# A decode step of attention and MLP: x and y made stationary for q and h, P widened to 64, a diagonal picked by masked sums, and `wo` loaded in 4-row runs

## The chip, the cores and the metric

The kernel runs on one core of a Trainium2 chip. The metric is the device time of one execution in microseconds, given as the median of the executions of a kernel with the lowest and the highest beside it. For a program on one core, "slow" is a run over 1.5% above the fastest of the same kernel.

## The reference, cut to what matters

Eight rows of one token each go through attention over the last 2048 positions of a cache (16 KV heads, two query heads each, 128 wide) and, beside it, through a GELU MLP; a sigmoid gate mixes the two.

```python
# x: 8 x 1 x 576; k_cache, v_cache: 8 x 16 x 8192 x 128; W = 2048; all bf16
q = x @ wq                                            # 576 x 4096
k, v = repeat(k_cache[:, :, Sk-W:]), repeat(v_cache[:, :, Sk-W:])
p = softmax(einsum("bhqd,bhkd->bhqk", q, k) * Dh**-0.5)
a = einsum("bhqk,bhkd->bhqd", p, v).reshape(...) @ wo   # 4096 x 576
b = gelu(layernorm(x) @ w1 + b1) @ w2 + b2            # 576 -> 4608 -> 576
return g * a + (1 - g) * b                            # g = sigmoid(sum(x * gate_w))
```

K and V in the window are 134 MB of the 154 MB that are read.

## The kernel before

One stream of loads on the sync engine fills nine slots of 2 MB in the order K, V, K, V, with four pieces of `wo` between and `w2` at the end. A K unit or V unit is one slot: four batch rows of one head. Four K units make a group with one softmax; there are eight groups. A K unit is transposed on VectorE in two halves, and each half feeds 8 matmuls on TensorE. A V unit does three things on TensorE's side: the PV matmuls, an eviction of their result by ScalarE, and a closing sum, which picks the useful diagonal out of the result.

A small planner inside the kernel fixes, at build time, the order of the instructions on every engine from modelled durations. On the chip each engine runs its own list in that order and waits at semaphores. The change and the argument touch these parts:

```python
def pv_fn(e):                                   # 16 matmuls, P stationary, 32 wide
    for t in range(16):
        c = 32 * (t % 4)
        mm = e.matmul(ps[c:c+32, BK_OS[i % 2], :], PT[...32*t : 32*t+32], slot(s)[:, 512*t:512*t+512], ...)
prev = add("pe", pv_fn, deps=[d] + pt_done[g] + [u_ev[i - 2]], cost=1.5, after=pv_hist[-1:])   # cut
u_ev[i] = add("act", ... activation(out=EV[:, i % 2, :], in_=ps[:, BK_OS[i % 2], :]), deps=[prev, u_sum[i - 2]])

def us_fn(e):                                   # closing sum: 4 fp32 matmuls on the diagonal blocks
    for r in range(4):
        mm = e.matmul(ps[...8 columns], EV[:, i % 2, 128*r:128*r+128], i32[:, 8*r:8*r+8], start=(r == 0), stop=(r == 3))
u_sum[i] = add("pe", us_fn, deps=[u_ev[i]] + ..., cost=1.0, prio=3)
# ...
# softmax of a group (cut): row maximum, exp, transposes of P, then
ds = add("dve", ... tensor_scalar(out=dsum, in0=i32, scalar1=k(S), op0=mult))       # 128 x 32
sp_ = add("pe", ... matmul(ps[:, BK_S, 0:32], ones_f, dsum))                        # sum of the group
# ...
d = dma("sp", ... A_wo[128*h0:128*(h0+8), :].rearrange("(t p) c -> p t c", p=128))  # rows of 1152 bytes
```

Of the kernel before, what the change touches and what calls it, by code (L numbers as in the profile page):

```python
# [179 lines left out]
def build_kernel(nc, A_x, A_k_cache, A_v_cache, A_wq, A_wo, B_x, B_w1, B_b1, B_w2, B_b2, gate_w, out):  # L180
# [16 lines left out]
    WOP = 768  # L197
# [7 lines left out]
    with ExitStack() as es:  # L205
# [19 lines left out]
        req("zeros_bf", 128, BF)  # L225
        req("maskL", 128, BF)
# [4 lines left out]
        req("sel", 4 * 128, BF)  # L231
        req("cols", 16, F32)
        req("xT", 6 * 8, BF)
        req("yT", 6 * 8, BF)
# [18 lines left out]
        req("EV", 2 * 512, F32)  # L253
        req("oT", Hkv * 16, BF)
        req("out_sb", JN, BF)
# [12 lines left out]
        over("sq", "KT", 2304, D, F32)  # L268
        arena = es.enter_context(nc.sbuf_tensor("arena", [128, (aoff[0] + 1) // 2], BF))
# [25 lines left out]
        sel = view("sel").rearrange("p (h c) -> p h c", h=4)  # L295
        cols = view("cols")
        xT = view("xT").rearrange("p (t b) -> p t b", b=8)
        yT = view("yT").rearrange("p (t b) -> p t b", b=8)
# [13 lines left out]
        o32 = view("o32").rearrange("p (u m) -> p u m", u=2)  # L312
        oT = view("oT").rearrange("p (u h b) -> p u h b", u=Hkv, h=2)
        out_sb = view("out_sb")
# [26 lines left out]
        BK_Q, BK_H, BK_X, BK_SEL = 4, 5, 6, 0  # L341
        BK_OS = (4, 5)
# [25 lines left out]
        o_selb = []  # L368
        for he in range(4):
            def fn(e, he=he):  # L370
                src = bass.AP(arena, offset=aoffs("ident") + 64 * (he // 2) + he % 2, ap=[[AST, 128], [0, 4], [2, 32]])
                return e.tensor_copy(sel[:, he, :].rearrange("p (a i) -> p a i", a=4), src)
            o_selb.append(add("pool", fn, deps=[o_ident], name="selb%d" % he, cost=0.3))
# [62 lines left out]
        def ev_T(dst, which):  # L436
            return lambda e: e.tensor_copy(dst, ps_bf[:, BK_X, which * 64: which * 64 + 48].rearrange("p (t b) -> p t b", b=8))
        o_xT = add("dve", ev_T(xT, 0), deps=[o_b1p], name="xT_ev", cost=0.2)
# [8 lines left out]
        o_yT = add("dve", ev_T(yT, 1), deps=[o_gp, o_yTp], name="yT_ev", cost=0.2)  # L447
# [6 lines left out]
        for q in range(4):  # L454
            o_i32.append(add("dve", (lambda q=q: lambda e: e.tensor_copy(i32[32 * q:32 * q + 32, :], ident[32 * q:32 * q + 32, 32 * q:32 * q + 32]))(),
                             deps=[o_ident, o_obl], name="i32_%d" % q, cost=0.15, prio=-1))


        def q_fn(e):
            ins = None  # L460
            for hq in range(Hq):
                out_ = ps[:, BK_Q, hq * 8: hq * 8 + 8]
                for t in range(4):
                    ins = e.matmul(out_, wq_m[:, t, hq * 128:(hq + 1) * 128], xT[:, t, :], start=(t == 0), stop=False)
                c = hq % 16
                ins = e.matmul(out_, wq_r[:, c * 128:(c + 1) * 128], xT[:, 4 + hq // 16, :], start=False, stop=True)
            return ins
        o_qp = add("pe", q_fn, deps=dwq + [o_xT], name="q_pe", cost=9.0)

        def qT_fn(e):  # L470
            src = bass.AP(ps, offset=BK_Q * 512, ap=[[PST, 128], [16, 16], [1, 8], [8, 2]])
            return e.tensor_copy(view("qT").rearrange("p (l b h) -> p l b h", l=16, b=8), src)
        o_qT = add("dve", qT_fn, deps=[o_qp], name="qT_ev", cost=0.4)

        def sel_fn(e):
            ins = None
            for he in range(4):
                ins = e.matmul(ps[:, BK_SEL + he // 2, (he % 2) * 256:(he % 2) * 256 + 256], sel[:, he, :], view("qT"), start=True, stop=True)
            return ins
        o_selp = add("pe", sel_fn, deps=[o_qT] + o_selb, name="sel_pe", cost=0.6, prio=9)  # L480

        def q4_fn(e):
            return e.activation(out=view("q4"), in_=ps[:, BK_SEL:BK_SEL + 2, :].rearrange("p a n -> p (a n)"), func=ACTF.Copy)
# [3 lines left out]
        H_CH = 6  # L487
        o_hch = []
        for i0 in range(0, FT, H_CH):
            fts = list(range(i0, min(FT, i0 + H_CH)))  # L490
            def fn(e, fts=fts):
                ins = None
                for t in fts:
                    c, j = divmod(t, FJ)
                    out_ = ps[:, BK_H, t * 8: t * 8 + 8]
                    for kt in range(4):
                        lhsT = bass.AP(arena, offset=aoffs("RAW") + W1O + kt * F + FCW * c + j, ap=[[AST, 128], [FJ, 128]])
                        ins = e.matmul(out_, lhsT, yT[:, kt, :], start=(kt == 0), stop=False)  # L498
                    lhsT = bass.AP(arena, offset=aoffs("RAW") + W1O + 4 * F + FCW * (c % 2) + j, ap=[[AST, 128], [FJ, 128]])
                    ins = e.matmul(out_, lhsT, yT[:, 4 + c // 2, :], start=False, stop=True)  # L500
                return ins
            o_hch.append(add("pe", fn, deps=dw1 + [o_yT], name="h_pe%d" % len(o_hch), cost=0.06 * 5 * len(fts), after=o_hch[-1:]))
        o_hp = o_hch[-1]

        def u_fn(e):
            in1 = bass.AP(arena_f, offset=foffs("b1T"), ap=[[AST // 2, 128], [1, FT], [0, 8]])
            return e.tensor_tensor(out=u_sb.rearrange("p (t b) -> p t b", b=8), in0=ps[:, BK_H, 0:FT * 8].rearrange("p (t b) -> p t b", b=8), in1=in1, op=ALU.add)
        GC = math.sqrt(2.0 / math.pi)
        o_u = add("dve", u_fn, deps=[o_hp, o_b1T], name="u", cost=0.45)
# [13 lines left out]
        def acc0_fn(e):  # L523
            ins = None
            for j in range(NJ):
                ins = e.matmul(ps[32 * j:32 * j + 32, BK_ACC, 0:JN], zeros_bf[:, 0:32], maskR[:, 0:JN], start=True, stop=True,
                               skip_group_check=True, tile_position=(0, 32 * j))
            return ins
        o_acc0 = add("pe", acc0_fn, deps=[o_z, o_mR], name="acc0", cost=0.5)
        acc_groups = []  # L530

        class AccGroup:
            def __init__(self, name, mms, deps, cost, after=(), prio=0):
                grp = self
                self.mms = mms

                def fn(e):
                    ins = None
                    for i, (lhsT, rhs) in enumerate(grp.mms):
                        for j in range(NJ):  # L540
                            ins = e.matmul(ps[32 * j:32 * j + 8, BK_ACC, 0:JN], lhsT, rhs[:, JN * j:JN * j + JN], start=False, stop=True,  # L541
                                           skip_group_check=True, tile_position=(0, 32 * j))
                    return ins
                self.op = add("pe", fn, deps=deps, name=name, cost=cost, after=list(after) + [o_acc0], prio=prio)
# [25 lines left out]
        u_ev, u_sum = {}, {}  # L570
        b6_w, b6_r = [], [o_yT, o_gb]
        proj_ops = {}
# [51 lines left out]
        def k_unit(i):  # L624
# [13 lines left out]
            for h in range(2):  # L638
# [23 lines left out]
                if q == 0 and h == 0:  # L662
                    deps += exp_done[g - 1] if g else [o_q4, o_mL, o_mR]
# [7 lines left out]
        def v_unit(i):  # L671
# [6 lines left out]
            def pv_fn(e):  # L678
                mm = None
                for t in range(16):  # L680
                    c = 32 * (t % 4)
                    mm = e.matmul(ps[c:c + 32, BK_OS[i % 2], :], PT[:, g % 2, 512 * q + 32 * t:512 * q + 32 * t + 32], slot(s)[:, 512 * t:512 * t + 512],  # L682
                                  start=(t < 4), stop=(t >= 12), skip_group_check=True, tile_position=(0, c))
                return mm
            deps = [d] + pt_done[g] + ([u_ev[i - 2]] if i >= 2 else [o_qT, o_u])
            prev = add("pe", pv_fn, deps=deps, name="pv%d" % i, cost=1.5, after=pv_hist[-1:])
            pv_hist.append(prev)
            slot_free[s] = [prev]
            if q == 3:
                pv_last[g] = prev  # L690
            u_ev[i] = add("act", lambda e: e.activation(out=EV[:, i % 2, :], in_=ps[:, BK_OS[i % 2], :], func=ACTF.Copy),  # L691
                          deps=[prev] + ([u_sum[i - 2]] if i >= 2 else []), name="uev%d" % i, cost=0.8, prio=3)

            def us_fn(e):
                mm = None
                for r in range(4):
                    mm = e.matmul(ps[:, BK_S, OC + 16 * (item % 2) + 8 * (q % 2):OC + 16 * (item % 2) + 8 * (q % 2) + 8], EV[:, i % 2, 128 * r:128 * r + 128], i32[:, 8 * r:8 * r + 8],  # L697
                                  start=(r == 0), stop=(r == 3), skip_group_check=True)
                return mm
            u_sum[i] = add("pe", us_fn, deps=[u_ev[i]] + o_i32 + b6_r[-2:], after=b6_w[-1:], name="us%d" % i, cost=1.0, prio=3)  # L700
# [18 lines left out]
        def wo_chunk(i):  # L719
            s = take_slot()  # L720
            h0 = WO_CH * i
            dst = slot(s)[:, 0:WO_CH * WOP].rearrange("p (t c) -> p t c", t=WO_CH)
            d = dma("sp", lambda e: e.dma_start(dst[:, :, 0:D], A_wo[128 * h0:128 * (h0 + WO_CH), :].rearrange("(t p) c -> p t c", p=128)),
                    "s%d" % s, WO_CH * 128 * D * 2, deps=slot_free[s], name="d_wo%d" % i, after=last_dma[-1:])
            last_dma.append(d)
# [112 lines left out]
```

## Time and profile before

The time was 369.55 us (369.44 to 369.65, three runs). The prediction shows the slices, the chain and the DMA stretches. In all profile lines PE is TensorE, PEld its weight loads, DVE VectorE, ACT ScalarE, POOL GpSimd and SP the sync engine; L691 is line 691 of the kernel that was run, so the same operation has another line number in each kernel.

Between a PV (L682) and its closing sum (L697) lies one eviction of 0.6 us, and TensorE hardly stands for it: 0.7 us at most. Its large waits are for the softmax (L606, the transposes of P) and for the transposed K (L642).

| | kernel before |
|---|---|
| busy of TensorE, VectorE, GpSimd | 72%, 57%, 10% |
| row maxima of groups 3 to 8 start at | 123.2, 165.1, 205.0, 246.4, 286.8, 328.3 us |
| that is, one group takes | 41.9, 39.9, 41.4, 40.5, 41.5 us |

### The profile page before, as it was taken

How to read it: one execution, taken by the hardware profiler on the slowest of the kernel's cores; microseconds unless marked ns; L12 is line 12 of the kernel's file. 1: busy time of each engine (PE TensorE's matmuls, PEld its weight loads, DVE VectorE, ACT ScalarE, POOL GpSimd, SP SyncE). 2: the span in 40 equal slices, each digit the busy share in tenths (PEclk: the TensorE clock that was granted, in tenths of full speed). 3: DMA queues.
4: the chain of work that ended last, by engine and by line, in shares of the span. 5: the costliest groups of instructions: out<-in, count | busy, mean ns of one | idle time of the engine just before them, and what ended most of it. 6: DMA issues, size and time to landing. Idle time of an engine off the chain costs nothing.

```text
span 367.9 us, 4129 instructions
## 1 busy us (share of the span) xinstructions
PE 263.5 (72%) x1837; PEld 87.0 (24%) x1429; DVE 210.4 (57%) x253; ACT 47.8 (13%) x117; POOL 37.5 (10%) x163
## 2 busy tenths in 40 slices
PE   0349984797698589773986399774976398773984
PEld 0339200122132022110321032110321032113542
DVE  0704599699686665459654674469544775364000
ACT  1010000210300220003000310003100300003200
POOL 7020011012011002000101002010110000000000
PEclk9999999699599869887897869886996879886659
DMA  8999999999999999999999999999999999999994
GB/s 345 428 412 424 435 430 433 428 428 428 433 429 431 422 433 426 428 435 427 433 431 433 408 434 432 429 426 433 433 436 428 414 434 424 431 433 440 402 429 193
DMA packets 14923, 154.59 MB, mean 420 GB/s; under 512 B 1292, under 2 KB 5428, under 8 KB 6072
## 3 DMA queue, kind: packets, MB, share of 16 engines
q1 hardware_dynamic: 14848, 154.29, 98.9%
q8 instruction: 13, 0.21, 0.2%
q10 hardware_dynamic: 56, 0.03, 0.0%
q14 instruction: 6, 0.05, 0.0%
HBM read 154.31 MB, written 0.01 MB: 419 GB/s over the span
## 4 chain that ended last, share of the span: by engine, by line
DMA 61%; PE 20%; DVE 16%; SPq 1%; issue 1%; ACT 0%; DVEq 0%; ACTq 0%
DMA arena<-in_A_k_cache_dram 50%; DMA arena<-in_B_w_dram 11%; DVE arena L642 10%; PE ps L173 9%; PE ps L659 3%; DVE arena L587 3%; PE ps L498 2%; PE ps L682 2%; PE ps L697 2%; DVE arena L606 1%; DVE arena L590 1%; PE ps L500 1%; SPq L675 1%; DVE arena L596 0%; SPq L746 0%
## 5 line engine op out<-in xcount | busy, mean ns | idle before, releaser
L642 DVE STREAM_TRANSPOSE arena<-arena 128x2048 f32<-128x2048 f32 x64 | 145.5, 2299 | 71.1 <-DMA arena<-in_A_k_cache_dram 60.1
L173 PE MATMUL ps<-arena 128*128 128x512 bf16 x408 | 141.3, 462 | 0.0
L659 PE MATMUL ps<-arena 128*128 128x512 bf16 x128 | 58.8, 459 | 21.4 <-DVE arena L642 21.3
L691 ACT ACTIVATE arena<-ps 128x512 f32<-128x512 f32 x32 | 19.1, 598 | 196.8 <-PE ps L682 196.8
L659 PEld LDWEIGHTS ps<-arena 128*128 128x128 bf16 x128 | 15.0, 117 | 124.6 <-issue 71.3
L635 POOL COPY arena<-arena 32x32 bf16<-32x32 bf16 x128 | 26.0, 203 | 159.8 <-PE ps L173 145.2
L697 PE MATMUL ps<-arena 128*128 128x8 f32 x256 | 35.3, 269 | 8.7 <-ACT arena L691 7.7
L697 PEld LDWEIGHTS ps<-arena 128*128 128x128 f32 x256 | 34.0, 208 | 21.8 <-ACT arena L691 15.2
L682 PE MATMUL ps<-arena 128*32 128x512 bf16 x512 | 36.4, 410 | 2.9 <-DMA arena<-in_A_v_cache_dram 2.9
L651 PE MATMUL ps<-arena 128*128 128x512 bf16 x8 | 4.7, 585 | 40.8 <-DVE arena L606 40.8
L587 DVE TENSOR_REDUCE arena<-ps 128x1 f32<-128x2048 f32 x8 | 18.3, 2282 | 21.6 <-PE ps L173 21.6
L601 ACT ACTIVATE arena<-ps,arena 128x512 bf16<-128x512 f32 x32 | 21.6, 686 | 40.9 <-DVE arena L596 40.9
L606 DVE STREAM_TRANSPOSE arena<-arena 128x512 bf16<-128x512 bf16 x32 | 19.9, 674 | 0.9 <-ACT arena L601 0.9
L682 PEld LDWEIGHTS ps<-arena 128*32 128x32 bf16 x512 | 11.3, 100 | 37.4 <-issue 27.1
L715 POOL TENSOR_TENSOR arena<-arena 128x16 bf16<-128x16 f32 x15 | 4.0, 266 | 141.7 <-ACT arena L707 141.7
L498 PE MATMUL ps<-arena 128*128 128x8 bf16 x144 | 10.9, 201 | 4.7 <-DMA arena<-in_B_w_dram 4.7
L541 PE MATMUL ps<-arena 128*8 128x288 bf16 (+1 forms) x140 | 11.9, 316 | 2.9 <-DMA arena<-in_B_w_dram 2.8
L498 PEld LDWEIGHTS ps<-arena 128*128 128x128 bf16 x144 | 10.8, 157 | 5.2 <-DMA arena<-in_B_w_dram 5.2
L651 PEld LDWEIGHTS ps<-arena 128*128 128x128 bf16 x8 | 0.9, 107 | 45.1 <-DVE arena L606 45.1
L613 DVE RECIPROCAL arena<-ps 128x32 f32<-128x32 f32 x8 | 2.9, 358 | 13.9 <-PE ps L611 13.9
L420 PE MATMUL ps<-arena 8*128 8x8 bf16 x8 | 0.5, 167 | 13.4 <-DVE arena L393 9.7
L715 DVE TENSOR_TENSOR arena<-ps,arena 128x16 bf16<-128x16 f32 x1 | 0.2, 229 | 16.7 <-PE ps L697 16.7
(83 smaller groups left out, 97.1 us busy)
## 6 DMA issues: line engine op xcount, KB each, us to landing
arena<-in_A_k_cache_dram SPq DMA_DIRECT2D x32, 2048.0 KB, 33.3
arena<-in_A_v_cache_dram SPq DMA_DIRECT2D x32, 2048.0 KB, 34.1
arena<-in_B_w_dram SPq DMA_DIRECT2D x1, 4608.0 KB, 24.3
arena<-in_A_wo_dram SPq DMA_DIRECT2D x4, 1152.0 KB, 36.6
arena<-in_A_wq_dram SPq DMA_DIRECT2D x1, 4096.0 KB, 13.0
arena<-in_B_w_dram SPq DMA_DIRECT2D x3, 1296.0 KB, 14.8
arena<-in_B_w_dram SPq DMA_DIRECT2D x2, 576.0 KB, 20.6
arena<-in_A_wq_dram SPq DMA_DIRECT2D x1, 512.0 KB, 3.6
```

The lines of the kernel that those rows point to most:

```text
L173: return e.add_instruction(mybir.InstMatmult(name=nc.get_next_instruction_name(), engine=mybir.EngineType.PE, ins=[e.lower_ap(rhs), e.lowe ...
L498: ins = e.matmul(out_, lhsT, yT[:, kt, :], start=(kt == 0), stop=False)
L541: ins = e.matmul(ps[32 * j:32 * j + 8, BK_ACC, 0:JN], lhsT, rhs[:, JN * j:JN * j + JN], start=False, stop=True, skip_group_check=True, til ...
L587: mx = add("dve", lambda e: e.tensor_reduce(out=k(MX), in_=ps[:, 0:4, :].rearrange("p a n -> p (a n)"), axis=AXL.X, op=ALU.max), deps=[qk_ ...
L601: return e.activation(out=Pm[:, 512 * c:512 * c + 512], in_=ps[:, c, :], func=ACTF.Exp, bias=k(NB), scale=SCALE, accum_out=k(SUM + c))
L606: pts.append(add("dve", (lambda c=c: lambda e: e.transpose(bass.AP(arena, offset=aoffs("PT") + 2048 * (g % 2) + 128 * c, ap=[[AST, 128], [ ...
L635: return e.tensor_copy(dst, src)
L642: tr = add("dve", (lambda h=h, kb=kb: lambda e: e.transpose(bass.AP(arena_f, offset=foffs("KT") + kb * 2048, ap=[[AST // 2, 128], [1, 2048]]),
L659: mm = e.matmul(*args, start=False, stop=last) if rc == 0 else held_matmul(nc, e, *args, stop=last)
L682: mm = e.matmul(ps[c:c + 32, BK_OS[i % 2], :], PT[:, g % 2, 512 * q + 32 * t:512 * q + 32 * t + 32], slot(s)[:, 512 * t:512 * t + 512], st ...
L691: u_ev[i] = add("act", lambda e: e.activation(out=EV[:, i % 2, :], in_=ps[:, BK_OS[i % 2], :], func=ACTF.Copy), deps=[prev] + ([u_sum[i - ...
L697: mm = e.matmul(ps[:, BK_S, OC + 16 * (item % 2) + 8 * (q % 2):OC + 16 * (item % 2) + 8 * (q % 2) + 8], EV[:, i % 2, 128 * r:128 * r + 128 ...
```

## The change

It means to take work off TensorE's instruction stream (fewer, wider matmuls for q, h, PV and the closing sum) and to load `wo` in longer runs. The core of the diff, with cuts marked:

```diff
 # q and h: x and y (x after layernorm) become the stationary operand, weights are streamed 512 or 288 wide
-            for hq in range(Hq): ... 5 matmuls, wq stationary, xT[:, t, :] moving
+            for t in range(5): for n in range(2): for j in range(4): ... xT stationary, wq moving
+        o_qx = add("dve", ... transpose of 128 x 1024 ...)
 # ... (h in the same way)
-                for t in range(16):   # PV: P 32 wide, V 512 wide, two banks in turn
+                for t0 in range(0, 8, 2): for dh in range(2): for t in (t0, t0 + 1):   # P 64 wide, V in two d halves
-            deps = [d] + pt_done[g] + [u_ev[i - 2]]
+            deps = [d] + pt_done[g] + u_ev[i - 1]        # both banks are used by every unit now
+            for dh in range(2): u_ev[i].append(add("act", ...))            # two evictions
+            re = "dve" if i >= NUQ - 3 else "pool"
+            um = add(re, ... EV * m8 ...)                                  # masked multiply, 128 x 1024 fp32
+            for n in (512, 256, 128): um = add(re, ... EV[0:n] + EV[n:2n])  # three adds (GpSimd only; VectorE: one strided reduce)
             def us_fn(e):
-                for r in range(4): ... EV block, i32
+                return e.matmul(..., E1[:, i % 2, :], s8)                  # one closing matmul
-    A_wo[...].rearrange("(t p) c -> p t c", p=128)
+    A_wo[...].rearrange("(g p t) c -> p g (t c)", g=2, t=4)                # runs of 4608 bytes
+    for hh in range(4): for t in range(4): ... add("dve", tensor_copy oT -> oTp)   # permutation, 16 per piece
```

## The prediction

> **What bounds the kernel now.** I read the page's slices first, then the chain that ended last, then the DMA rate in stretches around each load of `wo`, then the sync engine's issues and the last microseconds of the timeline.
>
> The slices of the page:
>
> ```profile
> span 367.9 us, 4129 instructions
> PE 263.5 (72%) x1837; PEld 87.0 (24%) x1429; DVE 210.4 (57%) x253; ACT 47.8 (13%) x117; POOL 37.5 (10%) x163
> ...
> DMA  8999999999999999999999999999999999999994
> GB/s 345 428 412 424 435 430 433 428 428 428 433 429 431 422 433 426 428 435 427 433 431 433 408 434 432 429 426 433 433 436 428 414 434 424 431 433 440 402 429 193
> DMA packets 14923, 154.59 MB, mean 420 GB/s; under 512 B 1292, under 2 KB 5428, under 8 KB 6072
> ```
>
> No compute engine is above 72%, while the 16 DMA engines are full from the first slice to the next to last. 154.59 MB at a steady 430 GB/s is 359.5 us; 2.2 us of start, 2 to 3 us of landing, last matmuls, eviction and store, and some slower slices make up the rest of 367.9. The bytes set the time; this change moves the same bytes.
>
> The chain seems to say otherwise:
>
> ```profile
> DMA 61%; PE 20%; DVE 16%; SPq 1%; issue 1%; ACT 0%; DVEq 0%; ACTq 0%
> ```
>
> It gives 36% to PE and DVE. That is how it walks: from a landing back to what freed the slot. While a slot is being freed, six or seven other loads wait in the queue (a K or V load takes a median 33.3 or 34.1 us from issue to landing, though 2 MB need 4.9 us). I take the DMA row as the verdict. Compute matters only if it uses up that lead: the shortest landings are 20.1 us for K and 16.2 us for V, so about 11 us are to spare even at the tightest place.
>
> The DMA rate in stretches (columns: stretch, length, busy of PE, PE loads, DVE, ACT, POOL with counts, clock, DMA share, GB/s):
>
> ```profile
> 90.00:124.00 34.00, 28.32 (x166) 7.61 (x115) 22.21 (x27) 4.84 (x13) 3.57 (x17) 0.80 1.01 431
> 124.00:135.00 11.00, 4.87 (x16) 0.45 (x4) 10.07 (x19) 3.38 (x9) 0.21 (x1) 0.73 1.02 417
> 135.00:205.00 70.00, 53.42 (x326) 15.00 (x235) 39.12 (x36) 7.71 (x19) 6.75 (x32) 0.85 1.01 430
> 205.00:217.00 12.00, 5.88 (x28) 0.91 (x15) 10.84 (x19) 3.38 (x9) 0.81 (x4) 0.75 1.04 423
> 217.00:286.00 69.00, 53.14 (x319) 14.92 (x227) 39.12 (x35) 7.71 (x19) 6.74 (x32) 0.85 1.00 429
> 286.00:300.00 14.00, 7.87 (x46) 1.70 (x37) 11.32 (x21) 3.38 (x9) 0.82 (x4) 0.76 1.03 424
> 300.00:340.00 40.00, 29.01 (x194) 10.29 (x145) 20.91 (x26) 6.03 (x15) 0.53 (x2) 0.84 1.01 431
> 340.00:353.00 13.00, 11.59 (x97) 7.14 (x97) 0.00 (x0) 2.76 (x6) 0.54 (x2) 0.63 1.02 416
> ```
>
> The four `wo` loads are issued at 95.7, 178.4, 259.9 and 314.8 us and land some 37 us later, in the four stretches of 416 to 424 GB/s. There the engines are as busy as elsewhere but move less: the cost of 1152-byte rows (4096 of the 5428 packets under 2 KB).
>
> The sync engine after the last `wo` issue, and the end of the chain:
>
> ```profile
> 314.83 0.37 SPq L723 DMA_DIRECT2D arena<-in_A_wo_dram  x1
> 315.25 0.53 SPq L735 DMA_DIRECT2D arena<-in_B_b_dram  x1
> 319.03 27.16 SPq L746 DMA_DIRECT2D arena<-in_B_w_dram  x1
> ```
>
> ```profile
> 348.46 16.55 DMA arena<-in_B_w_dram
> 365.06 0.43 PE ps L541 x4
> 365.61 0.45 DVE arena L764
> ```
>
> Behind each `wo` load one issue is held for 18 to 27 us: 1024 rows fill the queue. The queue stays full meanwhile, so this costs nothing. The end is the landing of the last `w2` piece, 0.43 us of matmuls, one eviction and the store.
>
> **What the Trainium skill says.**
>
> "DMA: Bandwidth & Descriptors", sections "Why small descriptors are slow (HBM only)" and "How a descriptor splits into AXI transactions": about 3 cycles of overhead per packet beside 32-byte beats, and a run that starts off a 256-byte boundary fetches from the boundary below. A 1152-byte row is 36 beats; every second row starts 128 B off, which makes it 40; with the overhead 41 on average, 1.139 of the ideal. Four rows in one run are 4608 B, 18 whole transactions: 147 for 144 beats, 1.021. A 16 KB K or V run is 515 for 512, 1.006. The trace agrees in sign and size (below).
>
> "GPSIMD Engine Reference", section "Performance versus the Vector engine": a two-input add of 2048 fp32 takes 4497 ns on GpSimd. This trace has only POOL's 128x16 multiply (266 ns), so it gives the fixed part and not the slope.
>
> "TensorEngine Tiling (Array Packing)", section "Performance Considerations": column tiles of 64 give a factor 2, of 32 a factor 4. The trace agrees for 32: 16 matmuls of 512 columns take 1.05 us at full clock, 66 ns each.
>
> "SBUF — State Buffer", section "Who interferes with whom": DMA never contends with a compute engine. The stretches agree: 429 to 431 GB/s outside the `wo` loads whatever DVE and PE do.
>
> **The change part by part.**
>
> `wo` in 4-row runs. 4.72 MB at 430 GB/s is 10.97 us. The loss today from the stretches against their neighbours: 11 x 13.5/430.5 = 0.34, 12 x 6.5/429.5 = 0.18, 14 x 6/430 = 0.20, 13 x 15/431 = 0.45, together 1.17 us. By the skill's beats it would be 10.97 x (1.139/1.006 - 1) = 1.45, and 0.16 would remain. I take the trace's figure less that rest: **-1.0 us**, on the path, because the DMA engines are the path.
>
> q and h with x and y stationary. q today: 17.02 to 21.45 us, 160 matmuls. After: 40 of 512 columns, four tiles at once, at 66 ns: 2.6 us. h today: 27.71 to 38.65, 10.9 us. After: 80 of 288 columns in 20 rounds, 20 x 288/512 x 0.26 = 2.9 us, plus a DVE transpose of 1152 fp32 (1.3 us from 2299 ns for 2048). Slots free 2 and 8 us sooner, QK starts about 5 us sooner, behind a queue that is full: **0**.
>
> PV. The fours become pairs: 8 rounds x 0.213 + 0.2 = 1.9 us a V unit at full clock (3.6 at half) in place of 1.05. The closing sum falls from 8 fp32 passes (1.06 us) to 2 (0.27). PE per unit 2.17 against 2.11: even. ACT evicts two banks, 2 x 0.6 in place of 0.6. POOL takes a masked multiply of 1024 and adds of 512, 256 and 128 for the first 29 units: 1920 elements at 2.2 ns plus four fixed parts near 0.2 (an estimate from the GPSIMD page) = 5.0 us a unit, 145 us in all, so POOL goes from 37.5 to some 180 us. Per K and V pair (9.8 us of DMA) POOL works 5.0 + 0.8: it fits. PV is single-buffered in PSUM now (waits for both evictions of the unit before): 1.9 + 1.4 = 3.3 us a unit, also inside 9.8. **0**.
>
> DVE. 64 permutation copies at 0.145 = 9.3 us, the sums of the last 3 units 3 x 2.4 = 7.3, two transposes 2.5: some 230 us, 62%. **0**.
>
> Instructions. PE loses about 410 matmuls and 750 weight loads; net about 900 of 4129. Instruction fetch has 0.26 MB and about 0.2% of the DMA time (0.7 us): **-0.15 us**.
>
> The tail. By bytes, V31 has landed 6.5 MB before the end of the loads: 363.3 - 15.1 = 348.2 us. P of the last group is transposed at 336.0; four PV units 3.3 to 5.0 us apart put the start of the last at 348 to 351. Then PV 1.9 to 3.6, evictions 1.4, multiply and reduce on DVE 2.4, sum 0.5, oT 0.3, waits 0.4, 8 late copies 1.3, projection of 16 matmuls 1.2 to 1.8: 357.5 to 363 us. The last `w2` pieces land from 363 to 365, so it fits, by little. If the static order puts the `w2` matmuls (1.3 us a chunk, three chunks) behind the projection, the end can slip by 1 to 2 us. I give it 15%: **+0.2 us**.
>
> Sum: 369.55 - 1.0 - 0.15 + 0.2 = **368.6 us**.
>
> **The rivals.**
>
> The tail becomes the bound: multiply, reduce, copies and projection of the last V unit outlast the last weights. For: it is a longer serial chain than today's and PE's clock is at half there (0.63 in 340 to 353). Against: 2 us or more of room in my sum. It would give 370 to 372.
>
> POOL becomes the pace. For: nothing here shows its fp32 rate; QK's small copies sit behind its sums in one in-order stream. Against: it would need about 9 us a V unit, near twice my estimate, before the pair's 9.8 us are full; each us beyond costs up to 29 us. That would be 378 or more; 3%.
>
> A real compute gain: the chain's 36% on PE and DVE shrinks and the kernel drops to 360 or below. Against: 154.6 MB at 430 GB/s are 359.5 us and nothing is moved less. 1%.
>
> The row length is hidden after all (the dips are the softmax and not `wo`): then no gain, 369.5. For: the dips fall near a softmax. Against: the softmaxes without a `wo` load, 164 to 176 and 246 to 258 us, ran at 429 and 430 GB/s (the same view), and the skill's beats give the same size.
>
> **Range and chances.** The first term is good to 0.4 us either way, the tail adds up to 2 us on one side: **367.6 to 370.2**. Two per cent is 7.4 us, which only the POOL rival or a mistake about the lead reaches: faster 1%, within 2% 96%, slower 3%.
>
> **What the profile after would show.** Packets under 2 KB near 1330, under 8 KB near 3000; no dip below 426 GB/s where `wo` lands; no issue held for 18 us and more behind `wo`. Matmuls near 1420 and weight loads near 680. h ends near 31 us. POOL near 180 us, no landing below 12 us, the DMA row still full. The chain still ends on a landing of `w2`, a few matmuls and the eviction; if it ends on the projection or the permutation copies, the tail rival won. A DMA slice below 9 in the middle, or POOL as the releaser in long waits of PE with landings of 6 us, would prove me wrong. If the dips stay with packets of 4608 B, the first term falls.

## More of the kernel before

The groups that make up one V unit (columns: line, engine, operation, tile, shape, count, then busy us and mean ns of one, then idle time ahead of them and what ended it):

```profile
L691 ACT ACTIVATE arena<-ps 128x512 f32<-128x512 f32 x32 | 19.1, 598 | 196.8 <-PE ps L682 196.8
L697 PE MATMUL ps<-arena 128*128 128x8 f32 x256 | 35.3, 269 | 8.7 <-ACT arena L691 7.7
L682 PE MATMUL ps<-arena 128*32 128x512 bf16 x512 | 36.4, 410 | 2.9 <-DMA arena<-in_A_v_cache_dram 2.9
```

A group is paced by its bytes: 205.1 us for five groups is 41.0 us each, and the DMA engines never pause.

TensorE's waits in the four middle groups (165 to 328 us; columns: who waited, for whom, us in total, times, the longest):

```profile
PE ps L651 <- DVE arena L606: 24.5, 4, 6.1
PE ps L659 <- DVE arena L642: 15.1, 10, 2.8
PE ps L697 <- ACT arena L691: 4.2, 6, 0.7
```

## The result, and the profile after

The changed kernel took **383.44 us** (379.25 to 387.6, four runs) against 369.54 for the kernel before on the same chip. The ratio is 1.034 (95% interval 1.026 to 1.042): slower, and far outside the predicted 367.6 to 370.2. Ratios here are the mean time of one kernel's fast runs over the mean of the other's fast runs of the same rounds, so they are not quite the quotients of the medians that are quoted. The profiled run is the slowest of the four (387.6 us, slow); it shows the effect in full size, and its granted clock (the share of TensorE's full clock that was granted) of 0.841 lies between those of the fast runs (0.839 to 0.860), so it is not a run at a lower clock.

The slices of the page:

```profile
span 385.9 us, 3257 instructions
...
PE 261.3 (68%) x1404; PEld 54.7 (14%) x683; DVE 242.4 (63%) x331; ACT 62.6 (16%) x149; POOL 163.5 (42%) x277
...
DMA  8999999999999999999999999999999999999400
GB/s 342 448 405 430 431 428 431 433 427 431 430 431 435 424 431 433 428 433 429 428 432 428 435 426 431 431 435 428 431 426 432 429 431 433 430 420 432 198 2 1
```

and the chain that ended last:

```profile
PE 32%; DVE 29%; DMA 16%; POOL 13%; issue 5%; ACT 3%; SPq 1%; POOLq 0%; DVEq 0%; ACTq 0%
```

The DMA row is as full as before until about 361 us, and then it falls to nothing: the loads end where they did, and the kernel goes on for 24 us without them. TensorE is *less* busy than before in share and in sum, so no engine ran out of throughput. The share of DMA in the chain fell from 61% to 16%.

The eight row maxima tell where the lateness comes in, since each ends the K half of a group:

| group | 3 | 4 | 5 | 6 | 7 | 8 |
|---|---|---|---|---|---|---|
| before, start us | 123.2 | 165.1 | 205.0 | 246.4 | 286.8 | 328.3 |
| after, start us | 124.0 | 166.8 | 212.4 | 257.0 | 301.2 | 345.8 |

At groups 3 and 4 the two kernels are level within 1.7 us. From there each group takes 44.7 us on average (179.0 us for four) in place of 40.8, and the last is 17.5 us late. That is the whole loss: the span grew by 18.0.

What TensorE waits for in those four groups (172 to 350 us) answers to TensorE's waits in the four middle groups of before:

```profile
PE ps L736 <- POOL arena L731: 23.3, 8, 4.0
PE ps L625 <- DVE arena L624: 19.0, 4, 5.2
PE ps L701 <- ACT arena L716: 5.1, 4, 1.3
PE ps L673 <- DVE arena L656: 2.4, 6, 0.6
```

L736 is the closing sum, L731 the last of GpSimd's adds. This row did not exist before: 5.8 us a group. The wait for transposed K (now L673 for L656) has all but gone, from 15.1 to 2.4: TensorE is behind the loads, and K lies ready when it arrives.

The groups of a V unit after, against the three lines of before:

```profile
L722 POOL TENSOR_TENSOR arena<-arena 128x1024 f32<-128x1024 f32 x29 | 55.0, 1897 | 71.2 <-ACT arena L716 70.8
L731 POOL TENSOR_TENSOR arena<-arena 128x512 f32<-128x512 f32 (+2 forms) x87 | 71.1, 817 | 6.8
...
L736 PE MATMUL ps<-arena 128*128 128x8 f32 x64 | 13.4, 285 | 33.5 <-POOL arena L731 26.7
```

The closing sums cost TensorE 13.4 us in place of 35.3, but TensorE stood still 33.5 us in front of them in place of 8.7. The 22 us of busy time saved here came back as 25 us of standing. PV itself took what was foreseen (236.08 to 238.00 us in the unit below: 1.92 for 1.9), and TensorE's busy time as a whole fell by only 2.2 us.

One V unit in the timeline shows the chain (columns: start, length, engine, what; in brackets the idle time before it and what ended it):

```profile
238.04 1.09 ACT L716 ACTIVATE arena<-ps 128x512 f32<-128x512 f32 x2 [7.32 <-PE ps L173]
...
239.26 1.90 POOL L722 TENSOR_TENSOR arena<-arena 128x1024 f32<-128x1024 f32 x1 [3.13 <-ACT arena L716]
...
240.87 0.84 PE L173 MATMUL ps<-arena 128*128 128x512 bf16 x3
241.23 2.61 POOL L731 TENSOR_TENSOR arena<-arena 128x512 f32<-128x512 f32 x3
...
243.89 0.39 PE L736 MATMUL ps<-arena 128*128 128x8 f32 x2 [2.19 <-POOL arena L731]
...
244.21 0.41 PE L701 MATMUL ps<-arena 128*64 128x512 bf16 x2
```

PV ends at 238.0. Two evictions (1.1), the multiply (1.9) and three adds (2.6) with their hand-overs put the closing sum at 243.89, that is 5.9 us later. TensorE's list has only one K unit in that gap (16 matmuls, done at 241.7), then the closing sum, then the next PV (244.21). So TensorE stands 2.19 us. Behind the next PV the list has only half a K unit, and TensorE stands 3.30 us. While TensorE is in step with the loads, this gap is filled for free: it would be waiting for K in any case. Once it is late, K is there at once, the matmuls on it take their bare length, and the chain sticks out.

### The profile page after: what moved, and what is told of

It is laid out like the page before. It is cut to its first block, busy times and chain, and to the rows that moved or that the text cites.

```text
span 385.9 us, 3257 instructions
## 1 busy us (share of the span) xinstructions
PE 261.3 (68%) x1404; PEld 54.7 (14%) x683; DVE 242.4 (63%) x331; ACT 62.6 (16%) x149; POOL 163.5 (42%) x277
## 2 busy tenths in 40 slices
DMA packets 11849, 154.53 MB, mean 400 GB/s; under 512 B 1292, under 2 KB 1332, under 8 KB 3000
## 4 chain that ended last, share of the span: by engine, by line
PE 32%; DVE 29%; DMA 16%; POOL 13%; issue 5%; ACT 3%; SPq 1%; POOLq 0%; DVEq 0%; ACTq 0%
PE ps L173 18%; DVE arena L656 14%; DMA arena<-in_A_v_cache_dram 9%; DMA arena<-in_A_k_cache_dram 8%; POOL arena L731 7%; POOL arena L722 6%; PE ps L701 4%; DVE arena L601 4%; PE ps L673 4%; DVE arena L620 3%; ACT arena L716 3%; PE ps L556 2%; PE ps L736 2%; DVE arena L624 2%; DVE arena L610 1%
## 5 line engine op out<-in xcount | busy, mean ns | idle before, releaser
L173 PE MATMUL ps<-arena 128*128 128x512 bf16 (+3 forms) x736 | 198.6, 442 | 8.6 <-DVE arena L528 4.4
L656 DVE STREAM_TRANSPOSE arena<-arena 128x2048 f32<-128x2048 f32 x64 | 145.7, 2298 | 35.4 <-PE ps L173 25.3
L722 POOL TENSOR_TENSOR arena<-arena 128x1024 f32<-128x1024 f32 x29 | 55.0, 1897 | 71.2 <-ACT arena L716 70.8
L731 POOL TENSOR_TENSOR arena<-arena 128x512 f32<-128x512 f32 (+2 forms) x87 | 71.1, 817 | 6.8
L701 PE MATMUL ps<-arena 128*64 128x512 bf16 x256 | 57.1, 439 | 18.5 <-DMA arena<-in_A_v_cache_dram 11.4
L716 ACT ACTIVATE arena<-ps 128x512 f32<-128x512 f32 x64 | 34.9, 598 | 160.9 <-PE ps L173 160.9
L673 PE MATMUL ps<-arena 128*128 128x512 bf16 x117 | 51.9, 444 | 8.5 <-DVE arena L656 8.5
L601 DVE TENSOR_REDUCE arena<-ps 128x1 f32<-128x2048 f32 x8 | 18.3, 2282 | 40.1 <-PE ps L173 40.1
L736 PE MATMUL ps<-arena 128*128 128x8 f32 x64 | 13.4, 285 | 33.5 <-POOL arena L731 26.7
L673 PEld LDWEIGHTS ps<-arena 128*128 128x128 bf16 x128 | 15.6, 122 | 104.3 <-issue 76.8
L701 PEld LDWEIGHTS ps<-arena 128*64 128x64 bf16 x256 | 16.5, 121 | 83.0 <-issue 64.1
L752 POOL TENSOR_TENSOR arena<-arena 128x16 bf16<-128x16 f32 x15 | 4.4, 291 | 38.3 <-ACT arena L744 38.1
L736 PEld LDWEIGHTS ps<-arena 128*128 128x128 f32 x64 | 12.0, 226 | 59.9 <-POOL arena L731 44.5
L625 PE MATMUL ps<-arena 128*128 128x32 f32 x16 | 3.9, 328 | 21.3 <-DVE arena L624 21.3
L665 PE MATMUL ps<-arena 128*128 128x512 bf16 x4 | 2.3, 586 | 11.5 <-DVE arena L620 11.5
## 6 DMA issues: line engine op xcount, KB each, us to landing
arena<-in_A_wq_dram SPq DMA_DIRECT2D x1, 4096.0 KB, 13.4
```

The lines of the kernel that those rows point to most:

```text
L173: return e.add_instruction(mybir.InstMatmult(name=nc.get_next_instruction_name(), engine=mybir.EngineType.PE, ins=[e.lower_ap(rhs), e.lowe ...
L601: mx = add("dve", lambda e: e.tensor_reduce(out=k(MX), in_=ps[:, 0:4, :].rearrange("p a n -> p (a n)"), axis=AXL.X, op=ALU.max), deps=[qk_ ...
L656: tr = add("dve", (lambda h=h, kb=kb: lambda e: e.transpose(bass.AP(arena_f, offset=foffs("KT") + kb * 2048, ap=[[AST // 2, 128], [1, 2048]]),
L673: mm = e.matmul(*args, start=False, stop=last) if rc == 0 else held_matmul(nc, e, *args, stop=last)
L701: mm = e.matmul(*args, start=(t < 2), stop=(t >= 6), skip_group_check=True, tile_position=(0, c))
L716: return e.activation(out=dst, in_=src, func=ACTF.Copy)
```

## The experiments

**The parts apart.** First PV and sums alone were set back, then done alone. All runs below passed the comparison with the reference, within its tolerance even the two that leave sums out, which are marked.

`no_pv`: the changed kernel with the PV part of before.

```diff
-  # P 64 wide, d halves, two evictions, masked multiply, adds, one closing matmul
+  # PV, eviction and four-matmul closing sum of the kernel before; q, h and wo as changed
```

> The changed kernel with the old PV and closing sums (32-wide P, two PSUM banks in turn, eight fp32 passes); q, h and wo as changed. Theory 1 (all of the loss comes from the PV part: PE waits in its fixed order for the masked sums on GpSimd, falls behind the loads and finishes late): 368.0 to 369.0 us, the gain of the wo runs visible, scatter of a few tenths. Rival (the permutation copies on DVE or the moved q and h cost something): above 371.

Measured 369.18 us (368.82 to 370.1, four runs), ratio 0.999 (0.998 to 1.001). The expectation's upper end was 369.0, so the size is off by a fifth of a microsecond; without the PV part there is no loss.

`pv_only`: the kernel before with the PV part alone.

```diff
-  # PV, eviction, closing sum of before
+  # P 64 wide, d halves, two evictions, masked multiply, adds, one closing matmul
```

> The kernel before with the PV part alone. Theory 1: 379 to 386 us with a scatter of some us, groups of softmax 44 to 45 us apart. Rival (the loss needs the other parts too, as the permutation copies that wait for GpSimd hold DVE): below 375.

Measured 374.87 us (370.71 to 380.84, four runs, one of them slow), ratio 1.011 (1.004 to 1.017). That is a miss: PV is necessary for the loss but brings only about a third of it alone, and the runs differ by 10 us.

**What of PV it is.** `pool_short` keeps every instruction and the planned order, and makes three of GpSimd's four operations short; the last add, over 128 elements, stays (a wrong sum).

```diff
-  x = EV[:, i % 2, :] ... in1 = m8 over 128 x 1024
+  x = EV[:, i % 2, 0:32] ... in1 = m8 over 128 x 32        # and the first two adds over 32 elements
```

> The changed kernel with the GpSimd sums cut to 32 elements each (wrong result on purpose), the planned order of all instructions unchanged. Theory 1: GpSimd's 4.5 us a unit and its hold on DVE's port are gone, so groups fall back to the pace of the loads (about 41 us) and the time to 369 to 374, what is left being the serial end behind the last loads. Rival (64-wide PV with one pair of PSUM banks, whose matmuls wait for two evictions, is the cost): stays at 379 or above.

Measured 369.02 us (368.88 to 370.0, four runs), ratio 0.999 (0.998 to 1.001). The length of GpSimd's work is what costs; the two evictions, the single-buffered PSUM and the 64-wide matmuls are all still there. This run can't tell whether the length costs TensorE directly or through VectorE, which long GpSimd operations hold up (below): that hold is gone here too.

`pool_half` asks for the dose: the multiply in full, the first two adds short (again a wrong sum).

```diff
-  add(in0=EV[:, i % 2, 0:n], in1=EV[:, i % 2, n:2*n])      # n = 512, 256
+  add(in0=EV[:, i % 2, 0:32], in1=EV[:, i % 2, 32:64])
```

> The changed kernel with the masked multiply in full and the three adds cut to 32 elements (a wrong result on purpose; same planned order): GpSimd's share of the chain from PV to closing sum falls from 4.4 to about 2.9 us. Latency theory: two or three closing sums a group lie in the open, so a late group loses 3 to 4 of its 44.5 us and comes to the pace of the loads (40.8): 368.8 to 374, last row maximum before 332. Rival (the stall comes with any GpSimd work between two TensorE steps, whatever its length): 379 or more.

Measured 369.47 us (368.31 to 371.57, twelve runs), ratio 1.001 (0.999 to 1.003): hit, last row maximum at 327.5. TensorE's waits from 172 to 328 us, the line for GpSimd:

```profile
PE ps L736 <- POOL arena L731: 5.4, 4, 2.5
```

TensorE still stands in front of four closing sums, for 1.4 us each instead of 2.9, and the kernel stays in step with the loads. Five of the twelve runs are at 370.2 to 371.6 and the others at 368.3 to 369.9.

**Length or place?** `us_late` gives GpSimd its full work and moves the closing sum in TensorE's list: behind the next PV instead of ahead of it.

```diff
             pv_hist.append(prev)
+            if i >= 1:
+                u_sum[i - 1].after.append(prev)       # order only, no new wait
```

> The changed kernel with each closing sum of a V unit placed on PE behind the next unit's PV, nothing else. Theory 1a (PE's fixed order is the cost, as PE stands still in front of the sum while GpSimd works): PE's waits for GpSimd go from 23 us in four groups to under 5, and the time to 370 to 375. Theory 1b (GpSimd holds the port that DVE's small operations need, so the softmax is late): the waits of the denominator's matmul stay near 5 us a group and the time stays above 378.

Measured 370.02 us (368.96 to 370.49, four runs), ratio 1.001 (0.999 to 1.003): hit. TensorE's longest waits from 172 to 328 us:

```profile
PE ps L673 <- DVE arena L656: 14.9, 12, 3.4
PE ps L173 <- DVE arena L620: 14.0, 2, 7.0
PE ps L665 <- DVE arena L620: 6.6, 1, 6.6
```

They are those of the kernel before again (transposed K, transposes of P), and no wait for GpSimd is left among those the answer lists. GpSimd does as much work as in the changed kernel (164.6 us against 163.5). So it is the order of TensorE's list, together with the length of the chain ahead of the closing sum, and not GpSimd's throughput.

The edit does more than its two lines say, because the planner plans every list anew. The changed kernel has, from the softmax of group 4 on, the matmul that sums the softmax (L625, which waits for VectorE) ahead of the first QK of the next group; `us_late` has it behind again, as the kernel before has. From the start of a row maximum to the next group's first QK (groups 4 to 7) pass 7.1 us before, 11.4 to 13.3 in the changed kernel and 7.1 to 9.1 in `us_late`. Group 6, changed kernel and then `us_late` (row maximum L601, sum L625, first QK L665):

```profile
257.00 2.29 DVE L601 TENSOR_REDUCE arena<-ps 128x1 f32<-128x2048 f32 x1 [12.48 <-PE ps L173]
...
267.47 0.63 PE L625 MATMUL ps<-arena 128*128 128x32 f32 x2 [4.60 <-DVE arena L624]
...
269.06 0.59 PE L665 MATMUL ps<-arena 128*128 128x512 bf16 x1
```

```profile
244.46 2.29 DVE L601 TENSOR_REDUCE arena<-ps 128x1 f32<-128x2048 f32 x1 [2.07 <-PE ps L173]
...
253.21 0.58 PE L665 MATMUL ps<-arena 128*128 128x512 bf16 x1 [6.61 <-DVE arena L620]
...
257.84 0.30 PE L625 MATMUL ps<-arena 128*128 128x32 f32 x2
```

No run was made for this rival, but the record bounds it. `pool_short` and `pool_half` keep the changed order (11.1 to 13.5 us) and lose nothing. `pv_only` and `no_wo` (below) have QK ahead in the step from group 6 to 7, and this step still takes 43.5 us in both, with 8.1 us of waits for GpSimd. TensorE's waits in that step of `no_wo` (254 to 297.5 us):

```profile
PE ps L737 <- POOL arena L732: 8.1, 4, 3.6
PE ps L666 <- DVE arena L621: 3.9, 1, 3.9
```

So this order alone does not make the loss; how much of the recovery in `us_late` it brings is not shown.

**The other parts.** `wo_only` is the kernel before with `wo` in 4-row runs and the permutation copies.

```diff
-  "(t p) c -> p t c", p=128                        # 1152-byte rows
+  "(g p t) c -> p g (t c)", g=2, t=4               # 4608-byte runs, and 64 copies on VectorE
```

> The kernel before with wo in 4-row runs and the permutation copies, nothing else. The prediction's first term: 1.0 us less, 368.5 to 368.7, with the DMA rate in the stretches where wo lands within 2 GB/s of its neighbours, and no issue held behind wo. Rival (the rate dips for another reason, or the end of the kernel eats the gain): 369.2 to 369.7; then the stretches say which of the two.

Measured **368.62 us** (368.42 to 369.94, eight runs), ratio 0.998 (0.997 to 0.999). It is the only version with a gain, and the best of all, if by 0.2% only. The stretches in which `wo` lands (same columns as in the prediction):

```profile
124.00:135.00 11.00, 5.68 (x18) 1.19 (x13) 9.20 (x20) 2.78 (x8) 0.00 (x0) 0.69 1.01 427
...
205.00:217.00 12.00, 7.39 (x46) 2.81 (x38) 9.14 (x21) 3.38 (x9) 0.00 (x0) 0.72 1.01 429
...
340.00:353.00 13.00, 11.60 (x97) 7.16 (x97) 1.28 (x8) 2.75 (x6) 0.54 (x2) 0.63 1.00 422
```

The dips of 417, 423, 424 and 416 GB/s became 427, 429, 427 and 422. Within 2 GB/s of its neighbours, as expected, is only the second, so part of the dip stays with the longer runs, most of it in the last stretch. In place of the issue that was held for 27.16 us behind the last `wo`, the longest one there now takes 4.2 us.

`no_wo` is the changed kernel with the old `wo`; `no_qh` is the changed kernel with the old q and h.

```diff
 # no_wo:  wo_chunk of the kernel before, no permutation copies
 # no_qh:  q_fn, h_fn and their evictions of the kernel before
```

> The changed kernel with wo as before, so without the permutation copies. By the theory of the copies: as PV alone, 371 to 376. By the theory of the start: as the changed kernel, 379 to 385.

> The kernel before with the PV and the wo part, q and h as before. If the permutation copies, which wait on DVE for GpSimd's results, add their stops to those of PE, this runs as the changed kernel: 379 to 385. If instead the earlier start of QK (q and h) pushes the kernel into its late rhythm, it stays near the kernel with PV alone: 371 to 376.

`no_wo` took 376.64 us (373.39 to 379.31, four runs, one slow), ratio 1.016 (1.012 to 1.020), just above what was expected. `no_qh` took 390.58 (378.68 to 391.17): above the expected 379 to 385. Three of its four runs count as slow against its one of 378.68, so no ratio is given. Taken alone, these two agreed with a rival: that the 64 permutation copies, which wait for GpSimd on VectorE, are the cost. `no_qh_late` tests it on the worst variant, with the copies left in and the closing sum moved as in `us_late` (with a new plan, as there).

```diff
 # no_qh, and:
+            if i >= 1:
+                u_sum[i - 1].after.append(prev)
```

> The changed kernel without its q and h part (the variant that took 390 us), with one thing more: TensorE's stream has each closing sum behind the next PV unit in place of ahead of it. Order theory (TensorE stands still in front of closing sums that are not ready): the stall goes here as it did for the whole change, 368.5 to 371 us, the last row maximum near 327, no wait of TensorE for GpSimd above 5 us in the four middle groups. Rival (the 64 permutation copies and the holds of VectorE by GpSimd cost time by themselves): they are all still there, so 376 or more.

Measured 369.46 us (368.52 to 370.62, twelve runs), ratio 1.000 (0.999 to 1.000), last row maximum at 327.5, one wait for GpSimd of 0.6 us. The copies cost nothing while TensorE is in step, so the rival falls. They can only have a say in when TensorE falls behind.

**A hold between two engines.** In the softmax of the changed kernel one small VectorE operation became slow: L624 (L610 before), 242 ns before and 954 on average after. The two engines in the timeline, VectorE and GpSimd:

```profile
265.81 1.60 DVE L624 TENSOR_SCALAR arena<-arena 128x32 f32<-128x32 f32 x1
```

```profile
265.48 1.90 POOL L722 TENSOR_TENSOR arena<-arena 128x1024 f32<-128x1024 f32 x1
```

It starts during GpSimd's multiply and ends with it (267.41 and 267.38). The Trainium skill, "SBUF — State Buffer", section "Who interferes with whom", says that VectorE with two SBUF inputs, or in one of its two-port modes, and GpSimd share one port pair, and that whoever comes second is blocked for the other's whole instruction. The trace agrees that the second one is blocked until the first ends; which of the two cases this is, it does not show. TensorE's second largest wait after (L625 for L624, 19.0 us) lies behind this operation, so the hold was a second rival. `ds_act` puts it on ScalarE and leaves the planned lists of TensorE, VectorE and GpSimd otherwise as they were.

```diff
-  ds = add("dve", ... tensor_scalar(out=dsum, in0=i32, scalar1=k(S), op0=mult))
+  ds on "act": activation(out=dsum, in_=i32, func=Copy, scale=k(S))     # moved after planning
```

> The changed kernel with one small operation of each softmax (128 x 32, the scaled identity ahead of the sum matmul; 954 ns on average on VectorE because GpSimd holds it up, 242 before) put on ScalarE, at its place in time; the planned order of TensorE, VectorE and GpSimd is the same. Hold theory (GpSimd's hold of VectorE in the softmax is the cause): 374 or less. Order theory (the hold only adds 0.7 us to each late group of 44.5, which stays above the 40.8 of the loads): 378 to 383, with the waits of TensorE for GpSimd as long as before.

Measured 376.92 us (375.71 to 388.11, six runs, one slow), ratio 1.022 (1.018 to 1.025). It lies between the two expectations, so both missed in size; the waits decided:

```profile
PE ps L744 <- POOL arena L739: 12.8, 6, 4.0
```

The longest wait for GpSimd (172 to 328 us) is still 4.0 us, and the two late groups still take 44.7 and 45.0 us. What changed is that TensorE fell behind two groups later. The excess of the three operations that GpSimd can hold in a softmax, over their mean times before (242, 192 and 147 ns), does not go with the time at all:

| variant | hold per group, us | time, us |
|---|---|---|
| changed kernel | 0.71 + 0.18 + 0.23 = 1.1 | 383.4 |
| `ds_act` | 0.71 + 0.65 = 1.4 (two operations left on VectorE) | 376.9 |
| `us_late` | 0.02 + 0.16 + 0.87 = 1.0 | 370.0 |
| `pool_half` | 0.27 + 0.30 + 1.03 = 1.6 | 369.5 |

In the last two TensorE is in step, so a hold may be hidden there. The hold is real and adds about 1 us to a softmax. It is not what makes a late group slow, but it has a say in when the lateness begins: with one of the three holds gone, the time fell from 383.4 to 376.9 us.

**The end.** `w2_first` tried to take 54 of the 70 matmuls that the changed kernel runs after its last closing sum out of the end, by ordering those of `w2` ahead of the last PV units and sums.

```diff
                 o_m2.append(ops[-1])
+            late = {0: pv_hist[30], 1: pv_hist[31], 2: u_sum[30], 3: u_sum[31]}[ci]
+            late.after.append(ops[-1])
```

> The changed kernel with the matmuls of w2 put on PE ahead of the last two PV units and sums instead of behind the projection. In the profiled run of the changed kernel 70 matmuls of 6.8 us stand at the very end although their weights landed 15 us earlier; 54 of them can go ahead. If the end is a chain of compute after a late softmax: 3 to 5 us less than the changed kernel, 378 to 381, and the softmaxes still 44 us apart. If the order at the end does not matter: 383.

Measured 387.21 us (382.87 to 388.45, four runs), ratio 1.044: a miss. The same matmuls now stood on the chain of the last V units, which was itself late. Moving work within that chain gained nothing.

What the variants have in common is seen in the time from one row maximum to the next (us; groups 3 to 8):

| variant | time | 3-4 | 4-5 | 5-6 | 6-7 | 7-8 |
|---|---|---|---|---|---|---|
| before | 369.5 | 41.9 | 39.9 | 41.4 | 40.5 | 41.5 |
| `us_late` | 370.0 | 39.8 | 39.9 | 40.4 | 41.1 | 41.7 |
| `pool_half` | 369.5 | 40.8 | 39.1 | 42.9 | 40.6 | 40.0 |
| `wo_only` | 368.6 | 42.3 | 38.0 | 45.6 | 38.1 | 41.2 |
| `pv_only` (profiled run 373.9) | 374.9 | 41.1 | 40.5 | 42.2 | 43.5 | 44.9 |
| `ds_act` (375.7) | 376.9 | 41.8 | 37.9 | 42.5 | 44.7 | 45.0 |
| `no_wo` (379.3) | 376.6 | 42.9 | 45.6 | 41.1 | 43.5 | 44.9 |
| changed kernel (387.6) | 383.4 | 42.8 | 45.5 | 44.6 | 44.2 | 44.6 |
| `no_qh` (391.1) | 390.6 | 43.3 | 45.5 | 44.6 | 44.2 | 44.6 |

There are two rhythms. In step with the loads a group takes about 41 us on average, whatever the variant; single ones scatter, as the 45.6 of `wo_only` with 38.1 behind it. Late, it takes 43.5 to 45.6 us, again whatever the variant. The one exception is the 41.1 of `no_wo`, a group in which TensorE waited for GpSimd once (4.0 us) and not twice (5.5 to 6.2 us in each late group of the changed kernel). As the late rhythm is slower than the loads, no kernel here that had fallen behind came back, and the loss is about 4 us for each group left. That fits the scatter: one and the same kernel, falling behind a group sooner or later, differs by 4 us a step. In the late groups of the changed kernel (166.8 to 345.8 us) TensorE is busy 31.3 us a group and stands for the rest. `us_late` removes from the late rhythm the 23.3 / 4 = 5.8 us a group of waiting for GpSimd; 44.7 - 5.8 = 38.9 us (an estimate from these two numbers) is faster than the loads, so a group that falls behind recovers.

What stays open is what makes TensorE fall behind in the first place, and why it happens sooner with the permutation copies and the old q and h. `pv_only` fell behind two groups before the end, `no_qh` already around group 4. No run separates the copies, the holds, the `wo` pieces and the order of the softmax's sum in this, and each of these variants was also planned anew.

## Why the prediction was wrong

The bound of the kernel before (its bytes) was read rightly, and so were most sizes: 1404 matmuls and 683 weight loads for 1420 and 680; the packet counts of 1332 and 3000 to the unit or nearly; GpSimd 163.5 us for 180, its work a V unit 1.9 + 2.5 = 4.4 us for an estimated 5.0.

- **The term for `wo`, -1.0 us: right.** `wo_only` gained 0.93 us by the medians. Three of the four dips rose above the 426 GB/s that the prediction named; the last stayed at 422.
- **q and h, 0: right as far as the runs can tell.** `no_pv`, which holds q, h and `wo`, is at 0.999 of before; beside `wo_only` it may have cost about half a microsecond.
- **PV, 0: the step that failed.** In the prediction's words: PV is "3.3 us a unit, also inside 9.8", and "Per K and V pair (9.8 us of DMA) POOL works 5.0 + 0.8: it fits." Both compare an engine's throughput with the pace of the loads. TensorE, however, meets GpSimd's work as a latency: 5.9 us from the end of PV to the closing sum, with 3.5 us of other matmuls between them in a fixed list. TensorE's standing adds 5.8 us to a group. The term was not 0: within the whole change it is about +14 us (383.44 against 369.18 in `no_pv`), alone about +5 (`pv_only`).
- **The POOL rival had the right engine and the wrong threshold.** It was dismissed because it "would need about 9 us a V unit". It took 4.4 us; 2.9 (`pool_half`) did no harm, and 4.4 did none either once the closing sum stood later (`us_late`).
- **"Compute matters only if it uses up that lead": the criterion itself was wrong.** The DMA row stayed full, and the shortest landing of V was 13.9 us, above the 12 that the prediction named as the limit. Both signs held, and the kernel was 4% slower. A lead of nine slots hides lateness from the loads; it does not hide it from the end, where what has been built up, 17.5 us, must still be computed after the last byte. The sign that did tell was the one about long waits of TensorE for POOL, but it had been tied to landings of 6 us.
- **DVE, 0.** The 64 copies at 0.17 us came out near the assumed 0.145, and cost nothing in step (`no_qh_late`). One size was off: multiply and strided reduce of the last three units took 1.23 + 1.90 = 3.1 us each in the trace of the changed kernel, for an assumed 2.4.
- **Instruction fetch, -0.15 us:** the kernel lost 872 of 4129 instructions, but no run isolates this.
- **The tail, +0.2 us: too small.** With the loss repaired, `us_late` is still 1.4 us above `wo_only` in the medians (ratios 1.0009 and 0.9979). Its chain ends on

```profile
359.01 6.45 PE ps L556 x70
```

70 matmuls behind the last closing sum instead of the landing of `w2`. That is the prediction's tail rival (1 to 2 us, given 15%), a likely reason for these 1.4 us, though no run takes this end alone away.

In sum, the change takes 22 us of busy time from TensorE's closing sums and puts a chain of 5.9 us through two other engines where one eviction of 0.6 us had been. The kernel was not bound by TensorE's busy time, so of this trade only the chain could show in the time. The best version found is the kernel before with `wo` in 4-row runs, 368.62 us; the full change with its closing sums one PV later is as fast as the kernel before and no faster.

## What to carry to other kernels

When a change hands a step to another engine, add up the latency from the producing instruction to the consuming one, and hold it against the work that lies between them in the consumer's own in-order list; throughput per unit of data is not enough. Then work out the pace of the loop for the case that all data is already there: if that pace is slower than the loads, the first disturbance is never made up, even though the DMA row stays full to the end. And when such a chain sticks out, first try to move the consumer one step later in its list: here two lines of ordering, and the new plan that they led to, gave back 13 us.

## What the Trainium skill lacked or had wrong

- "SBUF — State Buffer", section "Who interferes with whom", is right, and the prediction had used only its sentence on DMA. It gives no durations for small operations: here a 128 x 32 `tensor_scalar` on VectorE went from 242 ns to 954 on average and 1734 at most beside GpSimd's 1897 ns multiply, while the 32 x 1 `tensor_scalar` of the same softmax stayed at 144 ns in both kernels.
- "GPSIMD Engine Reference", section "Performance versus the Vector engine": its fp32 add of 2048 (4497 ns), scaled down in proportion, leaves 0.15 to 0.17 us an operation at the sizes here (1270, 726 and 454 ns for 512, 256 and 128; an estimate from that page). It says nothing of the multiply by a broadcast mask, which was quicker for its size: 1897 ns for 1024.
- "DMA: Bandwidth & Descriptors": by the beats as the prediction worked them out, the longer runs of `wo` save 1.45 - 0.16 = 1.3 us (an estimate from that page); 0.93 was measured. They do not account for the last stretch, which stayed at 422 GB/s with runs of 4608 bytes.
- On none of the pages used here did we find the main point: an in-order engine that falls behind a full load queue keeps a slower rhythm (44.7 us a group against 41) with the DMA row still at 9 of 10, and the loss shows only after the last byte.
